# The last 256 tokens of a Strassen-Winograd product computed plainly, in 256 columns instead of 128

## The chip, the cores and the metric

One NeuronCore of a Trainium2 chip runs the kernel; the other cores are idle. The metric is the device time of one execution in microseconds (us), lower is better. A few words used below: PE is TensorE (matmuls, into PSUM banks), PEld its weight loads, DVE is VectorE, ACT is ScalarE, POOL is GpSimd, and SP is the engine whose queue issues all DMA transfers here.

## What is computed

Attention with a feature map, then two MLPs on 2304 tokens (576 tokens of 4 batches). The change touches the second product of the second MLP alone:

```python
def _moe2_ref(x, w_in, w_out):
    h = np.maximum(x @ w_in, 0.0)
    return (h * h @ w_out).astype(np.float32)
# x: 2304 x 512, w_in: 512 x 2048, w_out: 2048 x 512, float32
```

So the output is `out = g @ w_out` with g = relu(x w_in)^2, 2304 tokens by 2048 hidden features, and w_out 2048 by 512.

## The kernel before

All of the work is recorded as operations with a key, a cost, reads, writes and buffers (`op`), and a planner (`Plan.run`) then writes one fixed order for every engine. Each engine executes its own order and waits on semaphores where an operand or a buffer isn't ready.

**fp32 by parts.** Every operand of a matmul is kept as a high part and a low part in the type fp32r: ACT casts the high part (`hi_act`, L430), DVE subtracts it to get the low part (`lo_on`, L434). A product of two 128 x 128 weight blocks with their data takes three matmuls: low weight x high data, high x low, high x high.

**The last product in seven.** `fold(i, q, key)` computes the part of out that belongs to token block i and to the pair q of 128-row chunks of the hidden features (q = 0 to 7). `BLOCKS` cuts the 2304 tokens into four blocks of 512 and a last one, i = 4, of 256. In each fold the work is a 2 x 2 by 2 x 2 block product in Strassen-Winograd form: the weights are split by output half (256 features each, A1x and A2x) and by chunk (Ax1 and Ax2), the data g by chunk and by token half. Seven products stand for eight. Their weight operands are A11 (product 1), A12 (product 2), A22 (product 4), and four sums of weights (3, 5, 6, 7; that of product 7 is A11 - A21). They are made once, for all blocks, by `w_sums` and `y_ahead`. The data operands are made in every fold: a load of g from DRAM (`load`, L1425 or L1430) into one of three `fold` buffers, four sums on DVE (`sums13` L1438, `sum2` L1443, `sum4` L1446), and the split of seven operands a, b, c, d into parts (tiles `ay` and `ghy`; `yb`; `yc`; `yd`).

**Columns.** A product has 6 matmuls (3 parts x 2 groups of 128 output features) and they stream half of the block's tokens: 256 columns in blocks 0 to 3, 128 columns in block 4. So a fold has 42 matmuls, and block 4 has 8 x 42 = 336 of 128 columns.

**Buffers.** The operand b of folds whose number k = 8 i + q isn't a multiple of three sits in one of two buffers (`rb`), the others in seven buffers that c and d use too (`xt`). The products of a block accumulate over q in one PSUM bank each (tile `y`), of eight banks.

**The end of a block.** After q = 7 the seven banks are combined: ACT copies product 1 (L1528), DVE does seven additions (`plus`, L1524), and SP stores four pieces of out (L1539). For block 4 this is the end of the kernel.

Of the kernel before, what the change touches and what calls it, by code (L numbers as in the profile page):

```python
# [13 lines left out]
ALU = mybir.AluOpType  # L14
# [15 lines left out]
NS, NQ = NTOK // S, NC // 2  # L30
# [244 lines left out]
def act(n, psum=False):  # L275
    return (51 if psum else 93) + 0.833 * n + 60


def dve(n, fast=False):
    return 70 + (0.52 if fast else 1.04) * n + 60  # L280
# [6 lines left out]
def dma(kb):  # L287
    return kb
# [15 lines left out]
def attention_then_two_mlps(ctx, tc, kT, qT, v, w_phi, w1, w2, out):  # L304
    nc = tc.nc
# [45 lines left out]
    gd = tc.dram_tile([128, NC, NTOK], F32, name="gd")  # L351
# [15 lines left out]
    op = plan.op  # L367
# [794 lines left out]
    accs = {}  # L1162
# [240 lines left out]

    def fold(i, q, key):
        at, cols = BLOCKS[i]
        half = cols // 2
        n = f"{i}_{q}"
        k = NQ * i + q
        Y = ("y", i, q)
        f = Buf("fx", None, None)  # L1410
        f.make = lambda: folds[f.home]
        of = [("gd", s, q, x) for s in range(at // S, (at + cols - 1) // S + 1) for x in range(2)]
        of += [(("xr", NS - 1), "lo", prod) for prod in SLOT]

        def part(x, a, b):
            if not folds:
                big = [
                    p.tile([128, 3, 4, 256], F32, tag="x", bufs=1, name=f"fold{x}") for x, p in enumerate((xp, late_pool()))
                ]
                folds.extend([[big[0][:, 0], big[0][:, 1]], [big[1][:, 0], big[1][:, 1]], [big[0][:, 2], big[1][:, 2]]])  # L1420
            return get(f)[x][:, a:b, :half]

        def load():
            if half == 256:
                nc.sync.dma_start(  # L1425
                    out=part(0, 0, 4).rearrange("p (c h) n -> p c (h n)", h=2), in_=gd[:, 2 * q:2 * q + 2, at:at + cols]
                )
                return
            for c in range(2):
                nc.sync.dma_start(  # L1430
                    out=part(0, 2 * c, 2 * c + 2),
                    in_=gd[:, 2 * q + c, at:at + cols].rearrange("p (h n) -> p h n", h=2),
                )

        op(key - 4, "SP", dma(cols), load, r=of, w=[(Y, "raw")], bufs=[f])

        def sums13():
            nc.vector.tensor_tensor(  # L1438
                out=part(1, 0, 2), in0=get(f)[0][:, 1:4:2, :half], in1=part(0, 0, 2), op=ALU.subtract
            )  # L1440

        def sum2():
            nc.vector.tensor_tensor(out=part(1, 2, 3), in0=part(0, 3, 4), in1=part(1, 0, 1), op=ALU.subtract)  # L1443

        def sum4():
            nc.vector.tensor_tensor(out=part(1, 3, 4), in0=part(0, 2, 3), in1=part(1, 2, 3), op=ALU.subtract)  # L1446

        tiles = {}

        def split(name, x, a, b, r):  # L1450
            if name == "a":
                t = g_tiles(NC * NL + NQ * NS + k, (F32R, F32R, F32), f"y{n}")
                both = lambda y: get(t)[y][:, :half].unsqueeze(1)
            elif name == "b" and k % 3:
                t = Buf("rb", None, None)

                def make(t=t):
                    if t.home == 0:
                        return [cp.tile([128, 2, 256], F32R, tag="c", name=f"yb{n}{y}") for y in range(2)]
                    b = rp.tile([128, 2, 2, 256], F32R, tag="raw", name=f"yb{n}")  # L1460
                    return [b[:, 0], b[:, 1]]

                t.make = make
                both = lambda y: get(t)[y][:, :, :half]
            else:
                t = wide("xt", (128, 2, 256), F32R, f"y{name}{n}")
                both = lambda y: get(t)[y][:, :, :half]
            tiles[name] = (t, both)

            def hi():  # L1470
                hi_act(both(0), part(x, a, b))

            def lo():
                lo_on("DVE", both(1), part(x, a, b), both(0))

            op(key, "ACT", act((b - a) * half), hi, r=r, w=[(Y, name, "hi")], bufs=[f, t])
            op(key, "DVE", dve((b - a) * half), lo, r=[*r, (Y, name, "hi")], w=[(Y, name)], bufs=[f, t])

        raw = [(Y, "raw")]
        split("a", 0, 0, 1, raw + [(("q", NS - 1, NQ - 1), "p1")])  # L1480
        split("b", 0, 2, 4, raw)
        op(key, "DVE", dve(cols), sums13, r=raw, w=[(Y, "t13")], bufs=[f])
        split("c", 1, 0, 2, [(Y, "t13")])
        op(key, "DVE", dve(half), sum2, r=[(Y, "t13")], w=[(Y, "t2")], bufs=[f])
        op(key, "DVE", dve(half), sum4, r=[(Y, "t2")], w=[(Y, "t4")], bufs=[f])
        split("d", 1, 2, 4, [(Y, "t4")])

        if q in AHEAD:
            W = lambda o: [(("ys", q), x, k) for x in range(2) for k in range(len(w_runs(3, q, x, 0, 7)))]
        else:  # L1490
            W = lambda o: [(("ys", q), "lo", o)]
        turn = [(("q", NS - 1, NQ - 1), "p7")]
        for prod, name, j in ((1, "a", 0), (6, "d", 0), (2, "b", 0), (5, "c", 0), (3, "b", 1), (7, "c", 1), (4, "d", 1)):
            if q == 0:
                accs["y", i, prod] = bank(f"y{i}_{prod}", None, "pb")
            acc = accs["y", i, prod]
            t, both = tiles[name]

            (hi, at0), (lo, at1) = (w_at(3, q, x, SLOT[prod]) for x in range(2))

            def mm(j=j, acc=acc, both=both, ws=((hi, at0), (lo, at1))):
                for d in range(2):
                    s = slice(d * 128, d * 128 + 128)
                    for x, (a, y) in enumerate(((1, 0), (0, 1), (0, 0))):
                        nc.tensor.matmul(  # L1505
                            get(acc)[:, d * 256:d * 256 + half], get(ws[a][0])[:, ws[a][1], s], both(y)[:, j],
                            start=q == 0 and d == 0 and x == 0, stop=q == NQ - 1 and x == 2, skip_group_check=True,
                        )

            o = 0 if prod in (1, 2) else 1 if prod == 4 else 2  # L1510
            op(key, "PE", 6 * (11 + half / 2.4), mm, r=[*W(o), (Y, name), *turn], w=[(Y, f"p{prod}")], bufs=[acc, t, hi, lo])
        if q < NQ - 1:
            return
        ab, cb = (
            Buf("ev", lambda x=x: rp.tile([128, 2, 2, 256], F32, tag="raw", name=f"ye{i}_{x}"), None) for x in range(2)
        )
        s1, u2, u4, c12 = ((lambda x=x, b=b: get(b)[:, x, :, :half]) for x in range(2) for b in (ab, cb))

        def bank_of(prod):
            return get(accs["y", i, prod]).rearrange("p (d n) -> p d n", n=256)[:, :, :half]  # L1520

        def plus(out, prod, y, r, w, bufs):
            def go():
                nc.vector.tensor_tensor(out=out(), in0=bank_of(prod), in1=y(), op=ALU.add)  # L1524

            op(key, "DVE", dve(cols), go, r=[(Y, f"p{prod}"), *r], w=w, bufs=[accs["y", i, prod], *bufs])

        op(key, "ACT", act(cols), lambda: nc.scalar.copy(out=s1(), in_=bank_of(1)), r=[(Y, "p1")], w=[(Y, "s1")],  # L1528
           bufs=[accs["y", i, 1], ab])
        plus(u2, 6, s1, [(Y, "s1")], [(Y, "u2")], [ab, cb])  # L1530
        plus(s1, 2, s1, [(Y, "s1"), (Y, "u2")], [(Y, "c11"), (Y, "s1")], [ab])
        plus(u4, 5, u2, [(Y, "u2")], [(Y, "u4")], [ab, cb])
        plus(c12, 3, u4, [(Y, "u4")], [(Y, "c12")], [ab, cb])
        plus(u2, 7, u2, [(Y, "u2"), (Y, "u4")], [(Y, "u3"), (Y, "u2")], [cb])
        plus(u4, 7, u4, [(Y, "c12"), (Y, "u4")], [(Y, "c22"), (Y, "u4")], [ab])
        plus(u2, 4, u2, [(Y, "u3")], [(Y, "c21"), (Y, "u2")], [cb])
        for d, h, t, r, b in ((0, 0, s1, "c11", ab), (0, 1, c12, "c12", cb), (2, 1, u4, "c22", ab), (2, 0, u2, "c21", cb)):
            def store(d=d, h=h, t=t):
                nc.sync.dma_start(out=out[:, d:d + 2, at + h * half:at + (h + 1) * half], in_=t())  # L1539

            op(key, "SP", dma(cols), store, r=[(Y, r)], bufs=[b])


    todo = []
# [28 lines left out]
    for i in range(1, NL):  # L1573
        for c in STREAM:
            at = key_of(i, c) - 0.5
# [3 lines left out]
    for c in range(NC):  # L1579
        for part in range(2):  # L1580
# [3 lines left out]
            at = base2 - W2A + W2B * (c if part == 0 else NC + c)  # L1584
            want(at, "key", second, at)
    for q in range(NQ):
        at = base2 - 13 + 2 * q
        want(at, "key", lambda key, q=q: w_sums(1, q, key), base2 + step * q - 1)
    for s in range(NS):
# [3 lines left out]
        for q in range(NQ):  # L1593
            at = base2 + (NQ * s + q) * step
            want(at, "key", lambda key, s=s, q=q: quad(s, q, key), at)
    for k, q in enumerate(AHEAD):
        at = base2 + NQ * step * P["ya"] + P["yb"] * k
# [64 lines left out]
```

## Time and profile before

| | us |
|---|---|
| time, median of 3 runs (989.99 to 990.82) | 990.0 |
| time of the profiled execution | 992.46 |
| its span, from the first to the last instruction | 990.7 |
| PE busy in the span | 972.5 (98%) |
| DVE busy | 764.4 (77%) |
| ACT busy | 620.6 (63%) |
| block 4's matmuls, 949.54 to 987.18 | 37.64 |

Starts are counted from the start of the span. A matmul's own duration in the trace is a latency (they overlap), so what one costs is read from the distance between starts. The profiled execution is 2.46 us above the median of the runs, 1.76 of it outside its span.

### The profile page before, as it was taken

The page shows a single profiled execution, that of the slowest core. Times are in us where ns is not written, and L with a number is a line of the kernel's source. Part 1 is how long each engine was busy: PE and PEld are TensorE (multiplying, and loading weights), DVE is VectorE, ACT ScalarE, POOL GpSimd, SP SyncE. Part 2 cuts the span into 40 slices and gives each one's busy share as a digit, 9 for nine tenths or more (in the row PEclk, how much of TensorE's full clock was granted, in tenths as well). Part 3 has the DMA queues.
Part 4 walks back from the last instruction along what each step waited for, and adds up shares of the span by engine and source line. Part 5 has one row for each costly group of instructions (what it writes and reads, how often), then busy time and mean ns, then how long its engine had stood idle before and what let it go on. Part 6 is the DMA issues. An engine that isn't in the chain of part 4 may idle for free.

```text
span 990.7 us, 18084 instructions
## 1 busy us (share of the span) xinstructions
PE 972.5 (98%) x6608; PEld 931.1 (94%) x6608; DVE 764.4 (77%) x1414; ACT 620.6 (63%) x1442; POOL 155.9 (16%) x132
## 2 busy tenths in 40 slices
PE   9969999999999999999999999999999999999998
PEld 6739999999999999999999999999999999999998
DVE  5999899777558867989766777785658999898753
ACT  6868778778678887866434445765656754444421
POOL 3140012200033000310000333241200430000000
PEclk9989999999999999999999999999999999999999
DMA  9548545464224654567557766673436945444320
GB/s 286 208 136 294 194 152 171 145 194 133 67 74 145 207 172 130 172 197 232 184 191 258 234 208 215 214 249 151 156 119 223 298 135 169 127 149 144 92 86 23
DMA packets 84531, 171.78 MB, mean 173 GB/s; under 512 B 15066, under 2 KB 41306, under 8 KB 77786
## 3 DMA queue, kind: packets, MB, share of 16 engines
q1 hardware_dynamic: 84442, 170.63, 52.5%
q8 instruction: 52, 0.85, 0.4%
q14 instruction: 37, 0.30, 0.1%
HBM read 123.77 MB, written 46.75 MB: 172 GB/s over the span
## 4 chain that ended last, share of the span: by engine, by line
PE 91%; DVE 6%; ACT 2%; issue 1%; DMA 0%; DVEq 0%; ACTq 0%
PE h L1180 20%; PE o L1219 20%; PE y L1505 19%; PE pb L1336 7%; PE pa L1336 5%; PE pc L1336 5%; PE pn L1101 4%; PE pk L844 3%; PE pkv L906 3%; PE pkv L952 3%; DVE w L434 1%; PE pq L1038 1%; PE pq L1039 1%; ACT kp L920 1%; DVE wc L566 1%
## 5 line engine op out<-in xcount | busy, mean ns | idle before, releaser
L1180 PE MATMUL h<-x,w 128*128 128x432 f32 (+1 forms) x1152 | 218.8, 340 | 2.3 <-DVE x L434 1.7
L1219 PE MATMUL o<-gh,w 128*128 128x432 f32 (+1 forms) x768 | 215.8, 339 | 0.0
L1180 PEld LDWEIGHTS h<-x,w 128*128 128x128 f32 x1152 | 198.3, 190 | 9.7 <-DVE x L434 2.1
L1219 PEld LDWEIGHTS o<-gh,w 128*128 128x128 f32 x768 | 139.9, 188 | 5.6 <-issue 1.7
L1219 PE MATMUL o<-gl,w 128*128 128x432 f32 (+1 forms) x384 | 130.1, 339 | 1.2 <-DVE gl L434 1.1
L1049 POOL PARTITION_ALL_REDUCE qm<-qp x32 | 75.4, 2374 | 268.0 <-ACT qp L1042 243.2
L1184 ACT ACTIVATE a<-h 128x432 f32<-128x432 f32 (+1 forms) x96 | 47.2, 493 | 80.1 <-PE h L1180 79.6
L1188 DVE SCALAR_TENSOR_TENSOR a<-a,h 128x432 f32<-128x432 f32 (+1 forms) x96 | 52.6, 549 | 43.2 <-ACT a L1184 42.6
L677 POOL TENSOR_TENSOR ws<-ws 128x256 f32<-128x256 f32 x56 | 52.7, 942 | 199.9 <-DVE wl L434 85.2
L1219 PEld LDWEIGHTS o<-gl,w 128*128 128x128 f32 x384 | 72.2, 188 | 3.4 <-DVE gl L434 1.7
L434 DVE TENSOR_TENSOR gl<-a,gh 128x432 fp32r<-128x432 f32 (+1 forms) x96 | 57.5, 599 | 15.0 <-ACT gh L430 13.9
L430 ACT CAST gh<-a 128x432 fp32r<-128x432 f32 (+1 forms) x96 | 49.7, 518 | 19.6 <-DVE a L1188 19.0
L1067 ACT ACTIVATE qe<-qp 128x576 f32<-128x576 f32 x64 | 42.1, 683 | 9.3 <-DVE qp L1055 8.4
L878 ACT ACTIVATE ke<-pk,mx 128x128 f32<-128x128 f32 (+1 forms) x160 | 44.2, 372 | 1.1 <-DVE x L1142 0.6
L849 DVE TENSOR_REDUCE mx<-pk 128x4 f32<-128x512 f32 (+1 forms) x48 | 28.3, 595 | 19.4 <-PE pk L844 19.1
L1101 PE MATMUL pn<-qh,kv 128*65 128x288 f32 x192 | 41.8, 294 | 0.0
L1505 PE MATMUL y<-yb,w 128*128 128x256 f32 (+1 forms) x270 | 39.5, 281 | 0.0
L952 PEld LDWEIGHTS pkv<-v,kp 128*128 128x128 f32 (+1 forms) x320 | 37.0, 191 | 2.3 <-issue 0.8
L434 DVE TENSOR_TENSOR qo<-qe,qh 128x576 fp32r<-128x576 f32 x48 | 35.7, 750 | 4.5 <-ACT qh L430 3.9
L952 PE MATMUL pkv<-v,kp 128*128 128x128 f32 (+1 forms) x320 | 38.9, 278 | 0.0
L1351 DVE TENSOR_TENSOR glq<-pb,aq 128x288 f32<-128x288 f32 x32 | 14.5, 455 | 28.7 <-PE pb L1336 28.7
L430 ACT CAST w<-ws 128x512 fp32r<-128x512 f32 (+2 forms) x36 | 23.7, 689 | 19.9 <-POOL ws L677 18.5
(424 smaller groups left out, 2716.6 us busy)
## 6 DMA issues: line engine op xcount, KB each, us to landing
w<-w1d SPq DMA_DIRECT2D x30, 1024.0 KB, 5.4
wbits<-w SPq DMA_DIRECT2D x16, 1024.0 KB, 5.3
wr<-w SPq DMA_DIRECT2D x32, 512.0 KB, 5.3
fold<-gd SPq DMA_DIRECT2D x32, 512.0 KB, 3.7
w2d<-wc SPq DMA_DIRECT2D x32, 256.0 KB, 4.1
qr<-qT SPq DMA_DIRECT2D x56, 144.0 KB, 3.3
ws<-w2d SPq DMA_DIRECT2D x28, 256.0 KB, 5.8
w1d<-w SPq DMA_DIRECT2D x6, 1024.0 KB, 4.5
```

What stands on the lines that cost most here:

```text
L430: nc.scalar.copy(out=dst, in_=src)
L434: e.tensor_tensor(out=dst, in0=src, in1=hi.bitcast(F32), op=ALU.subtract)
L677: nc.gpsimd.tensor_tensor(out=get(f)[:, o], in0=get(f)[:, a], in1=get(f)[:, b], op=how)
L952: nc.tensor.matmul(get(ps)[:, o:o + 128], get(kps[2 * g + s])[:nt, 2 * i + a], get(vt)[:nt, c:c + 128], start=t == 0 and a == 0 and s == 0 ...
L1049: nc.gpsimd.partition_all_reduce(get(mx), get(pr).rearrange("p a t -> p (a t)"), 128, bass.bass_isa.ReduceOp.absmax)
L1101: nc.tensor.matmul(get(ps)[:D1, :HB], w, get(e)[:, t], start=x == 0, stop=x == len(ops) - 1)
L1180: nc.tensor.matmul(get(ps)[:, :cols], a, x[:, cc, :cols], start=k == 0, stop=k == 3 * ND - 1)
L1184: nc.scalar.activation(out=get(gb)[0][:, :cols], in_=get(ps)[:, :cols], func=AF.Tanh, scale=0.5)
L1188: nc.vector.scalar_tensor_tensor(out=a, in0=a, scalar=1.0, in1=get(ps)[:, :cols], op0=ALU.add, op1=ALU.mult)
L1219: nc.tensor.matmul(get(acc)[:, :cols], a, g[:, :cols], start=c == 0 and x == 0, stop=c == NC - 1 and x == 2)
L1336: nc.tensor.matmul(get(ps)[:, :HB], ws[a][:, f], x[y][:, cc], start=first and k == 0, stop=k == 5, skip_group_check=True,)
L1505: nc.tensor.matmul(get(acc)[:, d * 256:d * 256 + half], get(ws[a][0])[:, ws[a][1], s], both(y)[:, j], start=q == 0 and d == 0 and x == 0, ...
```

## The change

For block 4 (`plain`, a block of under 512 columns) the fold no longer uses the seven products. It loads all 256 tokens of both chunks, splits the one operand b, and runs products 1, 2, 4 and 7 over 256 columns with the weight operands that were there: output half 1 is product 1 + product 2 (A11 B1 + A12 B2), and output half 2 is product 1 + product 4 - product 7 (A11 B1 + A22 B2 - (A11 - A21) B1). The other blocks run as before.

```diff
...
+        plain = cols < 512
+        half = min(cols, 256)
...
-            for c in range(2):
-                nc.sync.dma_start(
-                    out=part(0, 2 * c, 2 * c + 2),
-                    in_=gd[:, 2 * q + c, at:at + cols].rearrange("p (h n) -> p h n", h=2),
-                )
+            src = gd[:, 2 * q:2 * q + 2, at:at + cols]
+            if plain:
+                nc.sync.dma_start(out=part(0, 0, 2), in_=src)
...
+        if plain:
+            split("b", 0, 0, 2, raw)
+            products = ((1, "b", 0), (2, "b", 1), (4, "b", 1), (7, "b", 0))
+        else:
+            split("a", 0, 0, 1, raw + [(("q", NS - 1, NQ - 1), "p1")])
+            split("b", 0, 2, 4, raw)
+            op(key, "DVE", dve(cols), sums13, r=raw, w=[(Y, "t13")], bufs=[f])
...
-        for prod, name, j in ((1, "a", 0), (6, "d", 0), (2, "b", 0), (5, "c", 0), (3, "b", 1), (7, "c", 1), (4, "d", 1)):
+        for prod, name, j in products:
...
+        if plain:
+            plus(u2, 4, s1, [(Y, "s1")], [(Y, "u2")], [ab, cb])
+            plus(s1, 2, s1, [(Y, "s1"), (Y, "u2")], [(Y, "c11"), (Y, "s1")], [ab])
+            plus(u2, 7, u2, [(Y, "u2")], [(Y, "c21"), (Y, "u2")], [cb], ALU.subtract)
+            results = ((0, 0, s1, "c11", ab), (2, 0, u2, "c21", cb))
...
```

Up to block 4's first matmul the order of PE is the same in both programs. In the names below the first number is the block (`y4_1` is block 4's bank of product 1), and `wl3` and `w3` are the weights' parts. This is PE at the start of block 4, before:

```order
L1505 MATMUL y4_1_11817<-ay4_0_11631,wl3_1_9361 128x128
L1505 MATMUL y4_1_11817<-ghy4_0_11632,wl3_0_9265 128x128
L1505 MATMUL y4_1_11817<-ay4_0_11631,wl3_0_9265 128x128
L1505 MATMUL y4_1_11817<-ay4_0_11631,wl3_1_9361 128x128
L1505 MATMUL y4_1_11817<-ghy4_0_11632,wl3_0_9265 128x128
L1505 MATMUL y4_1_11817<-ay4_0_11631,wl3_0_9265 128x128
L1505 MATMUL y4_6_11828<-yd4_0h_11686,wl3_1_9361 128x128
L1505 MATMUL y4_6_11828<-yd4_0l_11687,wl3_0_9265 128x128
```

And this is the same place in the changed program:

```order
L1508 MATMUL y4_1_11771<-yb4_00_11654,wl3_1_9361 128x256
L1508 MATMUL y4_1_11771<-yb4_01_11655,wl3_0_9265 128x256
L1508 MATMUL y4_1_11771<-yb4_00_11654,wl3_0_9265 128x256
L1508 MATMUL y4_1_11771<-yb4_00_11654,wl3_1_9361 128x256
L1508 MATMUL y4_1_11771<-yb4_01_11655,wl3_0_9265 128x256
L1508 MATMUL y4_1_11771<-yb4_00_11654,wl3_0_9265 128x256
L1508 MATMUL y4_2_11779<-yb4_00_11654,wl3_1_9361 128x256
L1508 MATMUL y4_2_11779<-yb4_01_11655,wl3_0_9265 128x256
```

Each product still has six matmuls with a weight load each, now of 256 columns, and the fold goes on with products 4 and 7 instead of five others.

On DVE the program of before ends with block 4's last split and seven additions:

```order
L434 TENSOR_TENSOR yd4_7l_12203<-fold0_9095,yd4_7h_12202 128x2x128
L1524 TENSOR_TENSOR ye4_1_12250<-y4_6_11828,ye4_0_12242 128x2x128
L1524 TENSOR_TENSOR ye4_0_12242<-y4_2_11840,ye4_0_12242 128x2x128
L1524 TENSOR_TENSOR ye4_0_12242<-y4_5_11847,ye4_1_12250 128x2x128
L1524 TENSOR_TENSOR ye4_1_12250<-y4_3_11856,ye4_0_12242 128x2x128
L1524 TENSOR_TENSOR ye4_1_12250<-y4_7_11863,ye4_1_12250 128x2x128
L1524 TENSOR_TENSOR ye4_0_12242<-y4_7_11863,ye4_0_12242 128x2x128
L1524 TENSOR_TENSOR ye4_1_12250<-y4_4_11875,ye4_1_12250 128x2x128
```

The changed program ends on DVE like this, from block 3's last two additions on:

```order
L1530 TENSOR_TENSOR ye3_0_11728<-y3_7_11333,ye3_0_11728 128x512
L1530 TENSOR_TENSOR ye3_1_11737<-y3_4_11342,ye3_1_11737 128x512
L434 TENSOR_TENSOR yb4_31_11812<-fold0_9095,yb4_30_11811 128x512
L434 TENSOR_TENSOR yb4_5_11864<-fold0_9095,yb4_5_11864 128x512
L434 TENSOR_TENSOR yb4_61_11892<-fold1_9096,yb4_60_11891 128x512
L434 TENSOR_TENSOR yb4_7l_11895<-fold0_9095,yb4_7h_11894 128x512
L1530 TENSOR_TENSOR ye4_1_11991<-y4_4_11788,ye4_0_11977 128x512
L1530 TENSOR_TENSOR ye4_0_11977<-y4_2_11779,ye4_0_11977 128x512
L1530 TENSOR_TENSOR ye4_1_11991<-ye4_1_11991,y4_7_11797 128x512
```

Three wider additions take the place of seven, and the sum with product 2, whose result is stored on its own, stands between the sum with product 4 and the difference with product 7.

ACT's casts from block 3's last one to the end are these in the changed program (32 casts of block 4 before, 8 now):

```order
L430 CAST yd3_7h_11617<-fold1_9096 128x512
L430 CAST yb4_00_11654<-fold0_9095 128x512
L430 CAST yb4_1h_11663<-fold0_9095 128x512
L430 CAST yb4_4h_11712<-fold0_9095 128x512
L1534 COPY ye3_0_11728<-y3_1_11283 128x512
L430 CAST yb4_2_11760<-fold1_9096 128x512
L430 CAST yb4_30_11811<-fold0_9095 128x512
L430 CAST yb4_5_11864<-fold0_9095 128x512
L430 CAST yb4_60_11891<-fold1_9096 128x512
L430 CAST yb4_7h_11894<-fold0_9095 128x512
L1534 COPY ye4_0_11977<-y4_1_11771 128x512
```

The casts of folds 0, 1 and 4 now stand ahead of the copy that begins block 3's end, and one cast a fold is left.

## Rows read from the trace of the kernel before

**Rows 1.** The page: busy us (share of the span) and instructions of each engine.

```profile
PE 972.5 (98%) x6608; PEld 931.1 (94%) x6608; DVE 764.4 (77%) x1414; ACT 620.6 (63%) x1442; POOL 155.9 (16%) x132
```

**Rows 2.** The chain that ended last, from 900 us on: start, us, what.

```profile
899.90 87.28 PE y L1505 x756
987.18 0.03 issue
987.21 0.42 DVE ye L1524
```

**Rows 3.** Windows: length, busy by engine (instructions), granted clock, DMA share, GB/s.

```profile
929.64:949.54 19.90, 19.90 (x171) 19.90 (x169) 14.13 (x36) 7.18 (x18) 0.00 (x0) 1.00 0.20 61
949.54:987.18 37.64, 37.63 (x338) 37.49 (x336) 15.15 (x44) 7.86 (x22) 0.00 (x0) 1.00 0.16 47
```

**Rows 4.** Timeline of PE: block 3's folds 4 and 7, block 4's start and end.

```profile
929.64 0.28 PE L1505 MATMUL y<-ay,w 128*128 128x256 f32 x1
...
944.56 0.29 PE L1505 MATMUL y<-ay,w 128*128 128x256 f32 x1
...
949.54 0.23 PE L1505 MATMUL y<-ay,wl 128*128 128x128 f32 x1
949.60 0.27 PE L1505 MATMUL y<-ghy,wl 128*128 128x128 f32 x1
...
986.90 0.27 PE L1505 MATMUL y<-yd_7h,w 128*128 128x128 f32 x1
```

**Rows 5.** Timeline in block 4: weight loads and matmuls.

```profile
982.26 0.19 PEld L1505 LDWEIGHTS y<-ay,w 128*128 128x128 f32 x1
982.32 0.28 PE L1505 MATMUL y<-ay,w 128*128 128x128 f32 x1
982.37 0.19 PEld L1505 LDWEIGHTS y<-ghy,w 128*128 128x128 f32 x1
982.43 0.28 PE L1505 MATMUL y<-ghy,w 128*128 128x128 f32 x1
```

**Rows 6.** Groups by line and form, DVE from 936, ACT from 900 us: busy, mean ns.

```profile
L1524 DVE TENSOR_TENSOR ye<-y,ye 128x512 f32<-128x512 f32 x7 | 4.5, 685 | 0.4 <-ACT ye L1528 0.2
L1524 DVE TENSOR_TENSOR ye<-y,ye 128x256 f32<-128x256 f32 x7 | 2.8, 422 | 6.1 <-PE y L1505 6.1
L434 DVE TENSOR_TENSOR yd_7l<-fold,yd_7h 128x512 fp32r<-128x512 f32 x1 | 0.7, 691 | 0.9 <-ACT yd_7h L430 0.9
L430 ACT CAST yb<-fold 128x512 fp32r<-128x512 f32 x5 | 3.1, 618 | 2.9 <-PE y L1505 2.9
```

**Rows 7.** DMA issues by kind: count, KB each, median us to landing.

```profile
fold<-gd SPq DMA_DIRECT2D x32, 512.0 KB, 3.7
out<-ye SPq DMA_DIRECT2D x16, 256.0 KB, 2.3
fold<-gd SPq DMA_DIRECT2D x16, 128.0 KB, 2.2
out<-ye SPq DMA_DIRECT2D x4, 128.0 KB, 1.8
```

**Rows 8.** Timeline of ACT around block 3's end.

```profile
938.23 0.41 ACT L430 CAST yb<-fold 128x256 fp32r<-128x256 f32 x1 [2.38 <-PE y L1505]
939.11 0.41 ACT L430 CAST yc_0h<-fold 128x256 fp32r<-128x256 f32 x1 [0.47 <-DVE yb L434]
945.73 0.58 ACT L1528 COPY ye<-y 128x512 f32<-128x512 f32 x1
948.38 0.41 ACT L430 CAST yb<-fold 128x256 fp32r<-128x256 f32 x1 [2.08 <-issue]
```

**Rows 9.** Timeline of DVE: the ends of blocks 3 and 4.

```profile
946.34 3.48 DVE L1524 TENSOR_TENSOR ye<-y,ye 128x512 f32<-128x512 f32 x5 [0.19 <-ACT ye L1528]
950.07 1.28 DVE L1524 TENSOR_TENSOR ye<-y,ye 128x512 f32<-128x512 f32 x2
986.54 1.09 DVE L1524 TENSOR_TENSOR ye<-y,ye 128x256 f32<-128x256 f32 x3 [0.25 <-PE y L1505]
```

**Rows 10.** Timeline of SP's queue: the stores at the ends of blocks 3 and 4.

```profile
947.85 3.89 SPq L1539 DMA_DIRECT2D out<-ye  x4
984.98 3.23 SPq L1539 DMA_DIRECT2D out<-ye  x4
```

**Rows 11.** Who waited for whom on PE, from 800 us to the end.

```profile
PE y L1505 <- DVE yd_3l L434: 0.9, 1, 0.9
PE y L1505 <- DVE yc_4l L434: 0.6, 1, 0.6
```

More of the change, by code (lines that the diff above doesn't have):

```diff
@@ L1405, in fold @@
         at, cols = BLOCKS[i]
-        half = cols // 2
+        plain = cols < 512
+        half = min(cols, 256)
         n = f"{i}_{q}"
@@ L1423, in load @@
         def load():
-            if half == 256:
-                nc.sync.dma_start(
-                    out=part(0, 0, 4).rearrange("p (c h) n -> p c (h n)", h=2), in_=gd[:, 2 * q:2 * q + 2, at:at + cols]
-                )
-                return
-            for c in range(2):
-                nc.sync.dma_start(
-                    out=part(0, 2 * c, 2 * c + 2),
-                    in_=gd[:, 2 * q + c, at:at + cols].rearrange("p (h n) -> p h n", h=2),
-                )
+            src = gd[:, 2 * q:2 * q + 2, at:at + cols]
+            if plain:
+                nc.sync.dma_start(out=part(0, 0, 2), in_=src)
+            else:
+                nc.sync.dma_start(out=part(0, 0, 4).rearrange("p (c h) n -> p c (h n)", h=2), in_=src)
         op(key - 4, "SP", dma(cols), load, r=of, w=[(Y, "raw")], bufs=[f])
@@ L1479, in fold @@
         raw = [(Y, "raw")]
[L1480 to L1486, printed above, removed]
+        if plain:
+            split("b", 0, 0, 2, raw)
+            products = ((1, "b", 0), (2, "b", 1), (4, "b", 1), (7, "b", 0))
+        else:
+            split("a", 0, 0, 1, raw + [(("q", NS - 1, NQ - 1), "p1")])
+            split("b", 0, 2, 4, raw)
+            op(key, "DVE", dve(cols), sums13, r=raw, w=[(Y, "t13")], bufs=[f])
+            split("c", 1, 0, 2, [(Y, "t13")])
+            op(key, "DVE", dve(half), sum2, r=[(Y, "t13")], w=[(Y, "t2")], bufs=[f])
+            op(key, "DVE", dve(half), sum4, r=[(Y, "t2")], w=[(Y, "t4")], bufs=[f])
+            split("d", 1, 2, 4, [(Y, "t4")])
+            products = (
+                (1, "a", 0), (6, "d", 0), (2, "b", 0), (5, "c", 0), (3, "b", 1), (7, "c", 1), (4, "d", 1)
+            )
         if q in AHEAD:
@@ L1520, in bank_of, with plus @@
             return get(accs["y", i, prod]).rearrange("p (d n) -> p d n", n=256)[:, :, :half]
-        def plus(out, prod, y, r, w, bufs):
+        def plus(out, prod, y, r, w, bufs, how=ALU.add):
             def go():
-                nc.vector.tensor_tensor(out=out(), in0=bank_of(prod), in1=y(), op=ALU.add)
-            op(key, "DVE", dve(cols), go, r=[(Y, f"p{prod}"), *r], w=w, bufs=[accs["y", i, prod], *bufs])
-        op(key, "ACT", act(cols), lambda: nc.scalar.copy(out=s1(), in_=bank_of(1)), r=[(Y, "p1")], w=[(Y, "s1")],
-           bufs=[accs["y", i, 1], ab])
@@ L1530, in fold @@
[L1530 to L1537, printed above, removed]
+                a, b = bank_of(prod), y()
@@ new lines, in go @@
+                if how is not ALU.add:
+                    a, b = b, a
+                nc.vector.tensor_tensor(out=out(), in0=a, in1=b, op=how)
+            op(key, "DVE", dve(2 * half), go, r=[(Y, f"p{prod}"), *r], w=w, bufs=[accs["y", i, prod], *bufs])
+        op(key, "ACT", act(2 * half), lambda: nc.scalar.copy(out=s1(), in_=bank_of(1)), r=[(Y, "p1")], w=[(Y, "s1")],
+           bufs=[accs["y", i, 1], ab])
+        if plain:
[3 more added lines that the diff above has]
+            results = ((0, 0, s1, "c11", ab), (2, 0, u2, "c21", cb))
+        else:
+            plus(u2, 6, s1, [(Y, "s1")], [(Y, "u2")], [ab, cb])
+            plus(s1, 2, s1, [(Y, "s1"), (Y, "u2")], [(Y, "c11"), (Y, "s1")], [ab])
+            plus(u4, 5, u2, [(Y, "u2")], [(Y, "u4")], [ab, cb])
+            plus(c12, 3, u4, [(Y, "u4")], [(Y, "c12")], [ab, cb])
+            plus(u2, 7, u2, [(Y, "u2"), (Y, "u4")], [(Y, "u3"), (Y, "u2")], [cb])
+            plus(u4, 7, u4, [(Y, "c12"), (Y, "u4")], [(Y, "c22"), (Y, "u4")], [ab])
+            plus(u2, 4, u2, [(Y, "u3")], [(Y, "c21"), (Y, "u2")], [cb])
+            results = (
+                (0, 0, s1, "c11", ab), (0, 1, c12, "c12", cb), (2, 1, u4, "c22", ab), (2, 0, u2, "c21", cb)
+            )
@@ L1538, in store @@
+        for d, h, t, r, b in results:
             def store(d=d, h=h, t=t):
                 nc.sync.dma_start(out=out[:, d:d + 2, at + h * half:at + (h + 1) * half], in_=t())
-            op(key, "SP", dma(cols), store, r=[(Y, r)], bufs=[b])
+            op(key, "SP", dma(2 * half), store, r=[(Y, r)], bufs=[b])
     todo = []
```

## The prediction

> **What bounds the kernel now.** I read the page's busy times first: PE is busy for 972.5 of 990.7 us, 98%, and no other engine is above 77% [rows 1]. The share alone doesn't say what block 4 waits for, so next comes the chain that ended last. From 899.90 on it is one piece, 87.28 us of matmuls of the last product, and behind it only 0.03 us and one addition of 0.42 us on DVE [rows 2]. [...] So block 4 is bound by PE alone. What the change does to the time is what it does to the distance of PE's matmuls times their number, plus what it does behind the last matmul, as long as the operands still come in time.
>
> **What a matmul costs here.** A busy PE isn't PE at its peak, so the cost is the distance of the starts. In block 3, with 256 columns, fold 4 begins at 929.64 and block 4 at 949.54; between lie four folds of 42 matmuls: 19.90 / 168 = 118.5 ns each [rows 4]. In block 4, with 128 columns, the first matmul starts at 949.54 and the 336th at 986.90: 37.36 / 335 = 111.5 ns [rows 4]. Half the columns save 7 ns, 6%. The reason can be seen where weight loads and matmuls stand together: in block 4 the loads start at 982.26 and 982.37 and the matmuls at 982.32 and 982.43 [rows 5]. Both go at 0.11 us, and each matmul has a weight load of its own. So the narrow matmul is held by something that doesn't shrink with the columns, most likely its weight load, and the wide one nearly fits into the same time.
>
> [...]
>
> **The change part by part.**
>
> Matmuls: removed are 8 x 42 = 336 of 128 columns at 111.5 ns, 37.46 us. Added are 8 x 4 x 6 = 192 of 256 columns. Their cost is that of block 3's, the same line, shape, operands and number of weight loads: 192 x 118.5 ns = 22.75 us. The difference is -14.7 us. Bounds: at 111.5 ns for the wide ones, as if columns were free, 21.4 us and -16.1; from above, fold 7 alone gives (949.54 - 944.56) / 42 = 118.6 ns [rows 4], 0.02 us more in all. I take the mean over four folds, the same instruction in the same surroundings.
>
> Operands: each fold loses two loads of 128 KB, four sums and seven operands' splits, and gets one load of 256 KB, a cast of 0.62 us and a subtraction of 0.69 us [rows 6]. That is 8 x 0.69 = 5.5 us of DVE in some 23 us, less of a share than its 15.15 in 37.64 [rows 3]. I cost it at nothing, and the cover has to be shown, since a fold is now consumed in 24 x 118.5 ns = 2.84 us instead of 4.68. With block 4 starting at 949.54 as before, fold q starts at 949.54 + 2.84 q. The buffers of `rb` decide for folds 0, 2, 3, 5 and 6, as they hold one fold until its last product.
> - Fold 0's cast waited at 938.23 for PE to free that buffer [rows 8], and does so again: ready by 940.
> - Fold 2's takes the buffer of block 3's fold 7, as the cast at 948.38 did [rows 8]. Its subtraction stands behind five additions that end at 949.82 [rows 9], so it is ready at about 950.5 and wanted at 955.2.
> - Fold 3 reuses fold 0's buffer, free at 952.4: plus 0.62, 0.69 and some 0.2 of handing over it is ready at 953.9, wanted at 958.1. Fold 6 reuses that of fold 3, free at 960.9, and has the same 4 us to spare. Fold 5's buffer follows a store of block 3 and is free by 955.
> - Folds 1, 4 and 7 use `xt`, and there yc and yd no longer compete.
> - A load takes 3.7 us even at 512 KB [rows 7] and three `fold` buffers stand ahead. The last two loads are queued on SP behind stores of block 3, which ended at 947.85 + 3.89 = 951.74 [rows 10]; fold 6 is wanted at 966.6 and fold 7 at 969.4.
>
> So the nearest cover is 4 us, and if it were gone each of the two reuses would cost PE what exceeds it.
>
> The start of block 4: the casts of folds 1 and 4 now stand ahead of the copy that opens block 3's end, at 945.73 [rows 8]. Fold 1's can run at about 939.1, where the cast of yc_0h got a buffer, and fold 4's after its load (fold 1's subtraction at 940.4 plus 2.2 to 3.7 us [rows 7]), at about 943 to 944. That is before the copy, so block 3's banks come free as before, and product 2, 4 and 7 of block 4 find theirs (the additions of 946.34 to 949.82 [rows 9] have read them). If fold 4's cast came 3 us late, the copy would be late too and PE would wait about 1 us: I take nothing and keep 1 us for the range. PE's only two waits since 800 us, 1.5 us in all, are for block 0's operands [rows 11]; the changed stage asks less of the other engines than those that had none.
>
> The tail gets longer. Before, the last addition began 0.04 us after the last matmul's end and took 0.42 [rows 2]. Now product 4 ends 6 x 118.5 ns = 0.71 us before PE's end, then the three additions of 128x512 follow on DVE in a row: 0.69 us each [rows 6], at a distance of 0.60 to 0.70 [rows 9]. The last is a subtraction with the bank as its second operand, for which no row stands; the splits, subtractions too, take the same 0.69 [rows 6], so I take that. The first fills the time until PE's end, the other two end 1.3 to 1.4 us after it, against 0.46: +0.9 us (+0.8 to +1.0). The last store is then 256 KB instead of 128 KB, landing in 2.3 us instead of 1.8 [rows 7]: +0.5. The one before it, also 256 KB, is issued 0.7 us earlier; whether the two disturb each other the trace doesn't show at an end: between 0, as block 3's four stores within 3.89 us [rows 10] still had such a median, and the whole second transfer's extra 0.5 again. I take 0, since those are the nearest rows. The tail: +1.4 us (+1.2 to +2.0).
>
> The sum: -14.7 + 1.4 = -13.3 us. Against the profiled execution that is a span of 990.7 - 13.3 = 977.4 us, and 992.46 - 13.3 = 979.2 us of time. That execution was 2.46 us above the median, and the difference lies ahead of and around the stage; so the median goes from 990.0 to **976.7 us**.
>
> **The rivals.**
>
> PE goes by columns (the other side). Block 4 streamed 336 x 128 = 43008 columns and now streams 192 x 256 = 49152, 14% more: the seven products did save columns. If columns set the time, at the wide matmul's 118.5 / 256 = 0.463 ns a column, the 6144 more cost 2.8 us, and with the tail the time is 990.0 + 2.8 + 1.4 = 994.2 us. It decides if a narrow matmul costs less than (22.75 + 1.4) / 336 = 72 ns. Against it stands the measured 111.5 ns [rows 4]: 2%.
>
> [...]
>
> PE waits for operand b. If the chain from a freed buffer to a ready operand, 1.5 us by the rows, took more than 5.7 us (two folds), folds 3 and 6 would stall; at 8 us both lose 2.3 us: 976.7 + 4.6 = 981.3 us. The gain would be gone at 13.3 / 2 = 6.6 us of stall at each. For it: casts did wait for PE to free buffers [rows 8]. Against: 4 us to spare and DVE idle for most of the stage. 5%.
>
> The tail eats more, with stores that collide: at twice my +1.4 it gives 978.1 us. This stands inside the forecast's 90%, as some 10 of them.
>
> The change doesn't shorten the path because something else holds the end, a transfer or ACT: then 990 us. The chain has none from 900 us on [rows 2], and no transfer but the last stores is needed late: 1%.
>
> **How the numbers follow.** Forecast (a gain of 11.5 to 14.5 us, the two first bounds and a tail between +1.2 and +2.8): 90%. Waits for b with a gain of 2 to 11 us: 5%, and the like of it from an unseen buffer: 2%. No change 1%, columns 2%. A change of this kernel can be told from none at about 0.2%, 2.0 us. So faster 0.97, same 0.01, slower 0.02. The range: the sum's terms give 976.3 to 978.1; with 1 us for a late copy and half a microsecond for the runs' own spread (989.99 to 990.82) it is 975.6 to 978.6, which leaves 2 in 10 to the rest.
>
> **What would show it.** In the profile after, block 4's first matmul should stand at 949.5 and its last end near 972.4, the chain should hold 756 - 144 = 612 matmuls in about 72.5 us from 899.9 on, and the starts should lie 0.118 to 0.119 us apart. DVE's additions of the end should last until 1.35 us after it, and the last store should be 256 KB. I am wrong if the distance in block 4 is above 0.12, if PE shows waits for `yb` between 950 and 972, or if the span ends more than 5.6 us behind the last matmul (3.5 before).

## The result and the profile after

The changed kernel took 978.87 us (median of 4 runs, 975.73 to 979.02) against 990.0 us before (4 runs): a ratio of 0.9878, 95% interval 0.9858 to 0.9899. Five more runs of it gave a median of 978.16; over all nine it is 978.63, and over all 28 runs of before 990.0. The first median is 0.27 us above the range that was given, and the gain by these medians, 11.1 us, is below the forecast's 11.5 to 14.5.

The runs of either kernel lie at two levels by their mean granted clock, 2.3 and 2.6 us apart by the medians, though single runs of the two overlap (before, 991.46 us at 0.997 and 991.11 at 0.994). The traces show where it comes from: the clock between 50 and 80 us, long before the change begins. From 73 to 80 us it is 0.57 in before and after and 0.76 in e2_halves (means of 0.993 and 0.994), and 1.00 in e1_again, e3_cols128 and e4_p2_last (0.996). Block 4 starts at 949.54, 949.49 and 949.16 us in the first three, at 946.88 in e3_cols128, and at 946.36 and 946.75 in e5_w64 and e8_wide_w64, whose mean is 0.996 too. A comparison needs the level beside it. The table has the 24 runs of before with a clock on record; the first four have none.

| mean granted clock of the run | before, median us (runs) | after, median us (runs) | difference |
|---|---|---|---|
| 0.993 to 0.994 | 992.04 (10) | 978.90 (5) | -13.1 |
| 0.995 to 0.997 | 989.76 (14) | 976.30 (4) | -13.5 |

Both profiled executions had 0.993: 992.46 us before, 978.83 after, -13.6, and spans of 990.7 and 977.0.

Busy time by engine, from the page after (to be held against [rows 1]):

```profile
PE 957.8 (98%) x6464; PEld 916.1 (94%) x6464; DVE 751.3 (77%) x1362; ACT 614.3 (63%) x1418; POOL 156.0 (16%) x132
```

PE has 144 matmuls fewer and is busy for 14.7 us less; its share is the same 98%.

The chain that ended last, after, from 890 us on (start, us, what; the counterpart of [rows 2]):

```profile
889.94 81.83 PE y L1508 x690
...
971.86 0.70 DVE ye L1530
972.56 0.02 issue
972.58 0.69 DVE ye L1530
973.27 0.59 DVEq L1672
```

It is still one piece of matmuls. It leaves PE at 971.76, ahead of the last matmul, at the end of product 4, since the three additions on DVE now set the end.

Block 4 in the window of its matmuls after, line L1508 alone: length, PE busy, PEld busy, clock, DMA share, GB/s (compare [rows 3]):

```profile
949.49:972.46 22.97, 22.97 (x194) 22.76 (x192) 1.00 0.19 59
```

And its first and last rows in PE's timeline:

```profile
949.49 2.68 PE L1508 MATMUL y<-yb,wl 128*128 128x256 f32 x21
...
972.18 0.28 PE L1508 MATMUL y<-yb_7h,w 128*128 128x256 f32 x1
```

22.97 us stand where 37.64 stood, with no gap: 192 matmuls at (972.18 - 949.49) / 191 = 118.8 ns.

ACT's casts and copy around block 3's end, after (compare [rows 8]):

```profile
938.18 0.62 ACT L430 CAST yb<-fold 128x512 fp32r<-128x512 f32 x1 [2.76 <-PE y L1508]
...
943.87 0.62 ACT L430 CAST yb_4h<-fold 128x512 fp32r<-128x512 f32 x1 [3.92 <-DMA fold<-gd]
945.43 0.59 ACT L1534 COPY ye<-y 128x512 f32<-128x512 f32 x1 [0.94 <-PE y L1508]
...
952.45 0.62 ACT L430 CAST yb<-fold 128x512 fp32r<-128x512 f32 x1 [3.54 <-PE y L1508]
...
960.99 0.62 ACT L430 CAST yb<-fold 128x512 fp32r<-128x512 f32 x1 [6.35 <-PE y L1508]
```

Fold 4's cast came 1.5 us ahead of the copy, and folds 3 and 6 were cast at 952.45 and 960.99, as worked out (free at 952.4 and 960.9). PE's waits from 800 us on are the same two as in [rows 11]:

```profile
PE y L1508 <- DVE yd_3l L434: 0.9, 1, 0.9
PE y L1508 <- DVE yc_4l L434: 0.6, 1, 0.6
```

The end, from the timelines of DVE and SP's queue after (compare [rows 9, 10]):

```profile
971.86 1.42 DVE L1530 TENSOR_TENSOR ye<-y,ye 128x512 f32<-128x512 f32 x2 [8.92 <-PE y L1508]
973.19 0.68 DVE L1530 TENSOR_TENSOR ye<-ye,y 128x512 f32<-128x512 f32 x1
973.89 0.37 SPq L1554 DMA_DIRECT2D out<-ye  x1
```

The last matmul ends at 972.46, the last addition 1.41 us later, and the span 4.5 us later, against 3.5 before.

### The profile page after: what moved, and what is told of

The parts are those of the page before. It is cut to its first block, busy times and chain, and to the rows that moved or that the text cites. A ratio compares the mean times of both kernels' runs of the same rounds, so it can differ in the third digit from the quotient of the medians.

```text
span 977.0 us, 17669 instructions
## 1 busy us (share of the span) xinstructions
PE 957.8 (98%) x6464; PEld 916.1 (94%) x6464; DVE 751.3 (77%) x1362; ACT 614.3 (63%) x1418; POOL 156.0 (16%) x132
## 4 chain that ended last, share of the span: by engine, by line
PE 90%; DVE 7%; issue 1%; ACT 1%; DMA 0%; DVEq 0%; ACTq 0%
PE h L1180 21%; PE o L1219 20%; PE y L1508 17%; PE pb L1336 7%; PE pc L1336 5%; PE pa L1336 5%; PE pn L1101 4%; PE pk L844 3%; PE pkv L906 3%; PE pkv L952 3%; DVE w L434 1%; DVE wc L566 1%; PE pq L1038 1%; PE pq L1039 1%; DVE wc L562 1%
## 5 line engine op out<-in xcount | busy, mean ns | idle before, releaser
L1508 PE MATMUL y<-yb,w 128*128 128x256 f32 x316 | 44.7, 282 | 0.0
L1508 PEld LDWEIGHTS y<-yb,w 128*128 128x128 f32 x316 | 40.7, 189 | 0.0
```

What stands on the lines that cost most here:

```text
L1508: nc.tensor.matmul(get(acc)[:, d * 256:d * 256 + half], get(ws[a][0])[:, ws[a][1], s], both(y)[:, j], start=q == 0 and d == 0 and x == 0, ...
```

## The experiments

The theory: a matmul costs the longer of two things that overlap, its weight load (111.5 ns for 128 weight columns, whatever the data) and its stream of data. The change takes away 144 loads, and the wider streams, at 118.8 ns a matmul, nearly fit under those that are left. The main rival: PE goes by columns, or by a fixed cost an instruction.

**e1_again: the changed kernel once more.**

> The changed kernel once more, five rounds. Its first four runs gave 978.83, 978.90, 979.02 us at a mean granted clock of 0.993 and 975.73 us at 0.996. Theory chance: the clock early in the kernel takes one of two courses in either program, about 3 us apart, whatever stands at the end; then before shows both too (the profiled execution of before, 992.46 us, had 0.993) and at equal clock the gain is 13.5 to 14.5 us. Theory cost: the changed program falls to 0.993 by itself; then before stays near 990.0 at 0.996 in all runs, and 2.5 to 3 us of the gain are lost for good.

Measured: 978.16 us (975.52 to 979.44), before 990.73 in the ten runs beside it, ratio 0.9869 (0.985 to 0.9889). Before fell on both levels too (989.14 to 993.14), so the theory of chance holds; the table above has the levels. The gain at equal clock, 13.1 and 13.5 us, is below and at the lower end of the 13.5 to 14.5 that were expected. Windows of the changed kernel's first profiled execution (length, busy of PE, PEld, DVE, ACT, POOL, clock, DMA share, GB/s):

```profile
55.00:60.00 5.00, 1.92 (x4) 0.95 (x5) 4.70 (x6) 2.51 (x5) 5.00 (x4) 0.51 0.51 210
70.00:75.00 5.00, 3.16 (x13) 2.72 (x14) 4.91 (x10) 1.40 (x5) 0.00 (x0) 0.72 0.57 174
75.00:80.00 5.00, 5.00 (x20) 4.38 (x20) 4.89 (x14) 2.83 (x6) 0.00 (x0) 0.60 0.92 315
```

The same windows of this one, of the same program:

```profile
55.00:60.00 5.00, 2.77 (x6) 1.41 (x7) 4.70 (x5) 2.65 (x5) 5.00 (x3) 0.50 0.52 210
70.00:75.00 5.00, 3.61 (x22) 3.19 (x22) 4.92 (x8) 1.28 (x3) 0.00 (x0) 1.00 0.72 193
75.00:80.00 5.00, 4.76 (x33) 4.42 (x32) 4.87 (x16) 3.51 (x9) 0.00 (x0) 1.00 0.92 343
```

Both fall to about 0.5 near 55 us, where PE waits for operands (it is busy for 1.92 and 2.77 of the 5 us, and in the first waits 5.54 us ahead of its matmul at 58.08); only the first falls again near 73 us, and does 20 instead of 33 matmuls in the last of these windows.

**e2_halves: the plain scheme, but narrow.**

```diff
-                    for x, (a, y) in enumerate(((1, 0), (0, 1), (0, 0))):
+                    for h in range(2 if plain else 1):
+                        for x, (a, y) in enumerate(((1, 0), (0, 1), (0, 0))):
+                            o, n = d * 256 + h * 128, 128 if plain else half
...
+                                get(acc)[:, o:o + n], get(ws[a][0])[:, ws[a][1], s], both(y)[:, j, h * 128:h * 128 + n],
```

> Block 4 plain as in the change, but each matmul of 256 columns cut into two of 128 with a weight load each: 384 matmuls, 49152 columns, the same result. Theory fixed cost of a narrow matmul: 384 x 111.5 ns = 42.8 us against 22.75, so 20 us above the changed kernel, about 999 us, slower than before. Rival columns: the time of the changed kernel, within 1 us.

Measured: 997.67 us (995.06 to 998.71), ratio 1.006 (1.0039 to 1.0081): slower than before, and 19.0 us above the changed kernel's median of nine. Block 4's first and last rows on PE:

```profile
949.16 0.67 PE L1510 MATMUL y<-yb,wl 128*128 128x128 f32 x5
...
991.88 0.27 PE L1510 MATMUL y<-yb_7h,w 128*128 128x128 f32 x1
```

384 matmuls at 42.72 / 383 = 111.5 ns. The same columns and the same arithmetic, with twice the matmuls and loads, give the whole gain back and more. The rival of columns falls.

**e3_cols128: as many matmuls as in the change, half the columns.**

```diff
+                n = 128 if plain and q else half
...
-                            get(acc)[:, d * 256:d * 256 + half], get(ws[a][0])[:, ws[a][1], s], both(y)[:, j],
+                            get(acc)[:, d * 256:d * 256 + n], get(ws[a][0])[:, ws[a][1], s], both(y)[:, j, :n],
```

> Block 4 as in the change, but folds 1 to 7 stream only the first 128 of their 256 columns (half of the tokens' work is left out): 24 matmuls of 256 and 168 of 128 columns. Theory fixed cost: 168 x (118.5 - 111.5) ns = 1.2 us below the changed kernel. Rival columns: 168 x 128 x 0.463 ns = 10 us below it.

Measured: 975.97 us (975.04 to 976.73), 2.7 us below the median of nine; by level 1.1 us (975.2 against 976.3, higher clock) and 2.2 us (976.7 against 978.9). Folds 1 to 7:

```profile
949.76 0.22 PE L1509 MATMUL y<-yb_1h,w 128*128 128x128 f32 x1
...
968.36 0.28 PE L1509 MATMUL y<-yb_7h,w 128*128 128x128 f32 x1
```

168 matmuls at 18.60 / 167 = 111.4 ns, 7 ns less than with 256 columns: 1.2 us. The rest of the 2.7 is most likely scatter: runs of one level differ by up to 2.6 us (the changed kernel's at 0.995 to 0.996), and between 200 and 600 us e1_again's PE was busy for 399.17 of 400 us, e3's for all 400. Ten us, as by columns, are excluded.

**e5_w64: the kernel before with half the weight columns.**

```diff
+                m = 64 if i == 4 and q else 128
                 for d in range(2):
-                    s = slice(d * 128, d * 128 + 128)
+                    s = slice(d * 128, d * 128 + m)
...
-                            get(acc)[:, d * 256:d * 256 + half], get(ws[a][0])[:, ws[a][1], s], both(y)[:, j],
+                            get(acc)[:m, d * 256:d * 256 + half], get(ws[a][0])[:, ws[a][1], s], both(y)[:, j],
```

> The kernel before, with block 4's matmuls of folds 1 to 7 (294 of 336) on the first 64 of each weight block's 128 columns (half of those output features' work is left out); the data still have 128 columns. Theory weight load: what holds a narrow matmul at 111.5 ns is the load of 128 weight columns, so with 64 the distance falls to 56 to 80 ns and the time by 294 x (111.5 - 56 to 80) ns = 9 to 16 us, to about 975 to 981 us. Rival fixed cost: a matmul and its load cost 0.11 us to issue whatever their sizes, then nothing changes, within 1 us of the kernel before.

Measured: 975.26 us (974.76 to 976.92), before 990.33 beside it, 15.1 us less. A load, the matmuls at the start of fold 1 and at the end of fold 7:

```profile
951.00 0.13 PEld L1506 LDWEIGHTS y<-ghy,w 128*64 128x64 f32 x1
951.00 0.22 PE L1506 MATMUL y<-ay,w 128*64 128x128 f32 x1
...
968.62 0.22 PE L1506 MATMUL y<-yd_7h,w 128*64 128x128 f32 x1
```

294 matmuls at 17.62 / 293 = 60.1 ns, with the data as before. The rival of a fixed cost an instruction falls: the narrow matmul was held by the load of its 128 weight columns. By these distances a load takes 111.5 ns for 128 columns and at most 60.1 for 64.

**e8_wide_w64 and e9_cols64: which of the two holds which.** The first is e5's edit in the changed kernel (`m = 64 if plain and q else 128`). The second is the kernel before with e3's edit for 64 columns:

```diff
+                n = 64 if i == 4 and q else half
...
```

> The changed kernel with folds 1 to 7 of block 4 on 64 of 128 weight columns (half of those output features' work is left out), 256 columns of data. Theory two bounds: a matmul costs the longer of its weight load (111.5 ns for 128 columns) and its stream of data, and the wide one is held by its 256 data columns; then the distance stays at 117 to 119 ns. Rival: the load has a part in the wide one too (load and stream overlap only in part), then it falls to 108 to 112 ns.

> The kernel before with folds 1 to 7 of block 4 streaming 64 of their 128 columns (half of the tokens' work is left out), all weight columns. Theory two bounds: the weight load alone holds the narrow matmul, so the distance stays at 111 to 112 ns. Rival: it is the sum of a load and a part of the stream, as 0.060 us with 64 weight columns doesn't exclude, then it falls by 5 ns or more.

One execution each: 975.42 us, and 1018.28 us, against 989.03 for before beside them. The wide matmuls with 64 weight columns, folds 1 to 7 of e8_wide_w64:

```profile
949.27 0.28 PE L1509 MATMUL y<-yb_1h,w 128*64 128x256 f32 x1
...
968.76 0.28 PE L1509 MATMUL y<-yb_7h,w 128*64 128x256 f32 x1
```

19.49 / 167 = 116.7 ns, 2 ns below 118.8 and a little under what was expected: the wide one is held by its data almost alone. In e9_cols64 the matmuls of 64 columns begin like this:

```profile
953.64 0.28 PE L1506 MATMUL y<-ghy,w 128*128 128x64 f32 x1
...
956.99 0.28 PE L1506 MATMUL y<-yc_1l,w 128*128 128x64 f32 x1
```

30 matmuls later, 3.35 / 30 = 111.7 ns: half the data cost the same, as the theory has it. This also closes a gap in e5, whose edit halves the written output together with the weights: here the output is halved by columns and nothing is saved, so it is the load that counts. Then something came in that I hadn't expected; the windows of e9_cols64, columns as above:

```profile
953.60:956.00 2.40, 2.40 (x25) 2.40 (x23) 1.74 (x5) 0.70 (x2) 0.00 (x0) 1.00 0.50 137
957.00:958.00 1.00, 1.00 (x8) 1.00 (x7) 0.44 (x2) 0.40 (x1) 0.00 (x0) 0.57 0.11 31
960.00:1000.00 40.00, 40.00 (x190) 40.00 (x189) 6.07 (x20) 4.04 (x12) 0.00 (x0) 0.50 0.00 0
```

PE is busy without a gap, and its granted clock falls from 1.00 to 0.50 and stays there: 40 us for 190 matmuls, 0.21 us each. Block 4 takes 64.25 us instead of 37.64, which is 26.6 of the 29 us; the rest, 2.6, fits the start of block 4, at 948.92 us here and at 946.36 in e5_w64, the same program up to there, at 0.996; before beside it, at 0.995, most likely started it as early. It is a single execution: whether the fall comes in every run is not shown.

**e6_one_buffer: operand b without its cover.** Each fold of block 4 takes both `rb` buffers, so b has one.

```diff
...
-            elif name == "b" and k % 3:
+            elif name == "b" and (plain or k % 3):
                 t = Buf("rb", None, None)
+                if plain:
+                    more.append(Buf("rb", None, None))
...
```

> The changed kernel with one buffer for operand b in block 4 instead of two and the seven of xt, so that each fold's cast waits for the last matmul of the fold before. My working gives 0.62 + 0.69 us and 0.2 of handing over, 1.5 us of idle PE ahead of each of folds 1 to 7 and up to 1 ahead of fold 0: 10.5 to 11.5 us above the changed kernel, about 989. If PE's clock falls for the gaps the matmuls cost up to twice as much: above 1000 us. Rival: the operand comes late already in the changed kernel, which its trace doesn't show, then less.

Measured: 988.72 us (987.81 to 989.97), ratio 0.9984 (0.9974 to 0.9993), 10.1 us above the median of nine; by level 11.0 at the lower clock (989.9 against 978.9) and 12.3 at the higher (988.6 against 976.3), which is more than expected. In the traces, both at the lower level, block 4's last matmul ends 11.1 us later (983.56 against 972.46). PE at the starts of folds 1 and 2, with the idle time ahead:

```profile
953.98 0.38 PE L1510 MATMUL y<-yb,w 128*128 128x256 f32 x1 [0.59 <-ACT yb L430]
954.71 2.99 PE L1510 MATMUL y<-yb,w 128*128 128x256 f32 x23 [0.34 <-DVE yb L434]
958.29 0.38 PE L1510 MATMUL y<-yb,w 128*128 128x256 f32 x1 [0.59 <-ACT yb L430]
```

A fold takes 4.31 us instead of 2.84: 1.47 of waiting, first for the cast, then for the subtraction. My 1.5 us for the chain was right, and in the changed kernel it lies behind the other buffers. The clock stayed at 1.00 through these gaps (window from 949.5 to 982.9).

**e4_p2_last: the end reordered.**

```diff
-            products = ((1, "b", 0), (2, "b", 1), (4, "b", 1), (7, "b", 0))
+            products = ((1, "b", 0), (4, "b", 1), (7, "b", 0), (2, "b", 1))
...
-            plus(s1, 2, s1, [(Y, "s1"), (Y, "u2")], [(Y, "c11"), (Y, "s1")], [ab])
             plus(u2, 7, u2, [(Y, "u2")], [(Y, "c21"), (Y, "u2")], [cb], ALU.subtract)
-            results = ((0, 0, s1, "c11", ab), (2, 0, u2, "c21", cb))
+            plus(s1, 2, s1, [(Y, "s1"), (Y, "u2")], [(Y, "c11"), (Y, "s1")], [ab])
+            results = ((2, 0, u2, "c21", cb), (0, 0, s1, "c11", ab))
```

> The changed kernel with product 2 computed last in each fold and its sum added last, so that one addition of 128x512 instead of two follows the last matmul. My sum has 0.7 us of the tail in the second one: 0.6 to 0.7 us below the changed kernel at equal clock. Rival: the end is set by the two stores, which then come closer together or in another order: no change within 0.3 us.

Measured: 976.49 us (975.86 to 977.23), ratio 0.9857 (0.9839 to 0.9875). At the higher level its three runs are around 976.2 against 976.3, at the lower its one run is 977.23 against 978.9: the times alone don't settle it. The trace does:

```profile
970.73 0.28 PE L1508 MATMUL y<-yb_7h,w 128*128 128x256 f32 x1
...
971.08 0.68 DVE L1530 TENSOR_TENSOR ye<-y,ye 128x512 f32<-128x512 f32 x1
971.79 0.37 SPq L1554 DMA_DIRECT2D out<-ye  x1
```

From the last matmul's end at 971.01 to the end of the span at 974.9 are 3.9 us, against 4.5 in the changed kernel and 4.6 in e1_again: the second addition's 0.7 us. By its trace it has the shortest end of all versions with the full result, by less than a total can show.

**e7_two_halves: the last sum in two halves.** On top of e4_p2_last, product 2's sum and store are cut by output group.

```diff
...
+                    nc.vector.tensor_tensor(out=s1()[:, d], in0=bank_of(2)[:, d], in1=s1()[:, d], op=ALU.add)
...
+                    nc.sync.dma_start(out=out[:, d, at:at + cols], in_=s1()[:, d])
...
```

> The changed kernel with product 2 last, and its sum made and stored in two halves of 128x256. In the trace of product 2 last, 3.9 us lie behind the last matmul instead of 4.6. Now the last addition ends 0.1 us later, but its store is 128 KB, which landed in 1.8 instead of 2.3 us before: 0.2 to 0.4 us less, 3.5 to 3.7 us behind the last matmul, the time about 1 us below the changed kernel at equal clock. Rival: what remains behind the last store doesn't depend on its size: 3.9 to 4.0 us.

Measured: 976.55 us (975.65 to 977.36). Its end on PE, DVE and SP's queue:

```profile
971.00 0.28 PE L1508 MATMUL y<-yb_7h,w 128*128 128x256 f32 x1
971.35 0.75 DVE L1542 TENSOR_TENSOR ye<-y,ye 128x256 f32<-128x256 f32 x2
971.94 0.89 SPq L1545 DMA_DIRECT2D out<-ye  x2
```

4.1 us from the last matmul to the end, not 3.5 to 3.7: wrong. The additions end at 972.10, but the two stores are issued one after the other until 972.83, so the second leaves later than it could, and they landed in 2.1 us, not 1.8.

## Why the prediction was right, and where it wasn't

**The matmuls.** 37.64 us became 22.97: -14.67 against -14.7. The distance of block 3's matmuls held in block 4 (118.8 for 118.5 ns). That a narrow matmul is held by its weight load was only likely from the rows; e5 shows it, e9's first microseconds show that 64 data columns cost what 128 do, and e2 that the columns alone would have made the change a loss.

**The operands.** Costed at nothing, rightly: no wait of PE in block 4, the casts at the worked-out times, and 1.47 us a fold when e6 takes the cover away.

**The tail.** The mechanism was right and one term too big: +1.0 us instead of +1.4. The additions gave +0.95 (1.41 us behind the last matmul instead of 0.46), as said. The +0.5 for the landing of a larger store was the mis-sized term. The last two stores of before on SP's queue:

```profile
987.32 0.88 SPq L1539 DMA_DIRECT2D out<-ye  x2
```

The second of them, 0.42 us long, is issued at 987.79, 0.16 us after its addition ended at 987.63, with the first, ahead of it in the queue, ending at 987.69; after, the last store left 0.02 us behind its addition. From the last store's issue to the end of the span it is 2.9 us with 128 KB (before) and 3.1 with 256 KB (after), so the size cost 0.2 us and not 0.5, and the wait that went away gave most of it back: from the last addition to the end it is 3.1 us in both. e7 agrees: 3.0 us from the issue of its last store of 128 KB (972.44) to the end.

**The sum.** -13.3 was forecast; at equal clock level -13.1 and -13.5 were measured, and the span is 977.0 for 977.4. The step that failed is the last one: "the median goes from 990.0 to 976.7". It put the 2.46 us by which the profiled execution stood above the median ahead of the stage, rightly, but took them for a property of that execution alone. The section on the time before puts 1.76 us of them outside the span, and that is a misreading: time and span are 1.7 to 1.9 us apart in every run (989.14 and 987.4, 978.83 and 977.0), so the 2.46 us lie inside the span, ahead of block 4. They are a level on which runs of either program fell, 10 of 24 before and 5 of 9 after. Three of the first four runs after were on the lower clock; the first four before have no clock on record, but their times (989.9 to 990.82) are nearer to the higher level (989.76) than to the lower (992.04). That it was three of four was chance: of all nine it is five. The range had half a microsecond for the runs' spread where 2.5 were wanted. Nor is its upper edge the sum that it names: 978.1, 1 us for a late copy and half a microsecond make 979.6, not 978.6, and 978.87 would have lain inside.

**The rivals.** Columns: excluded by e2, e3 and e5. Waits for b: not there. A tail at twice its price: it was smaller instead. The gain of 11.1 us by the first medians lies where the forecast ends and the waits for b begin, but it is the clock level and no such wait: PE shows none.

## What to carry to other kernels

A scheme that saves columns by making matmuls narrower pays only while the stream of data is longer than the weight load: here 256 columns cost 118.8 ns, 128 cost 111.5 and 64 still 111.7. In these traces both are even a little under 256 columns (an estimate from 111.5 ns for the load of 128 weight columns and 116.7 ns for 256 data columns), so below that what counts is the number of loads. A shorter stage is worth what its new tail doesn't take back: look at what follows the last matmul, addition by addition, and at how many stores queue on one engine. And before a difference of one per cent is split into terms, look at whether single executions of one kernel differ by a good part of that somewhere else.

## What the runs showed of the hardware that was not expected

The granted clock fell to 0.50 while PE was busy in every window: matmuls of 64 data columns with loads of 128 weight columns (e9_cols64, one execution): 1.00 in the window from 953.6 to 956.0 us, 0.57 from 957 to 958, then 0.50 to the end. It didn't fall in block 4 for 128 data columns with the same loads (before), nor for 64 weight columns at 60 ns (e5), nor in e6 with 1.47 us of waiting in each 4.31: there it stayed at 1.00. What brought it down is not shown. At 0.50 a matmul with its load took 0.21 us instead of 0.11, and the load's own time in the trace was 0.33 us (at 1004.80) instead of 0.19 (at 948.92); since the load held the matmul at 0.11, the load goes by that clock too.

In the early part, which these programs share, the clock fell once or twice. The fall near 55 us is in before, after and e1_again to e4_p2_last alike: 0.51 to 0.63 from 55 to 62 us. In e1_again, e3_cols128 and e4_p2_last it begins earlier (0.98 to 0.99 over the first 55 us, in e1_again 0.84 from 50 to 55), and from 73 to 80 us the clock is 1.00. In before, after and e2_halves the first 55 us are at 1.00 and the clock falls again near 73 us, to 0.57, 0.57 and 0.76 from 73 to 80. Both kinds occur in runs of one and the same program (after and e1_again), and some 2.5 us hang on it, 2.3 and 2.6 by the medians of the two levels; what decides between them is not shown.
